# Blocks of attention scores in larger parts where the instruction stream is crowded, and an earlier index for the last batch's left tiles

## The chip, the core and the metric

The kernel runs on one core of one Trainium2 chip. The metric is the device time of one execution in microseconds, lower is better. TensorE (PE; its weight loads are shown as PEld), VectorE (DVE), ScalarE (ACT), GpSimd (POOL) and SyncE (SP, which issues most DMAs) each run their own instructions in program order and wait for each other on semaphores.

## The reference

Agent attention feeds a top-1 mixture of experts, in float32:

```python
def _attn_ref(q, k, v, agents):          # q, k, v: 4 x 11456 x 128, agents: 4 x 49 x 128
    a2k = sm(agents, k)                  # softmax of scaled scores
    agent_v = a2k @ v
    q2a = sm(q, agents)
    return q2a @ agent_v
...
def _moe_ref(x, w_gate, w_output_gate, w1, w2):   # x: 45824 x 128, 8 experts, F = 1024
    logits = x @ w_gate
    e_idx = np.argmax(logits, axis=1)
...
    gate_w = probs[np.arange(N), e_idx]
    eom = 1.0 / (1.0 + np.exp(-(x @ w_output_gate)))
    for e in range(E):
        mask = e_idx == e
...
        h = np.maximum(x[mask] @ w1[e], 0.0)
        ye = h @ w2[e]
        out[mask] = gate_w[mask, None] * eom[mask, e, None] * ye
```

## The kernel before

The tokens of each of the four batches are cut into 12 units (`UNITS`): 11 of 8 times 128 tokens and one of 2 times 96. For every unit there are score products of q with the 49 agents (tiles qs), and of k (ks); with their softmax weights the agents' averages of v are built per batch (ev, av), and from these one expert is chosen for the batch. The main loop then multiplies, for tiles of 512 tokens, the turned attention weights (x_ld) by first-layer weights folded with the averages (h), takes the relu in two float16 halves (hh by ACT, hl by DVE), multiplies by the second layer (y), and DVE or ACT with POOL scales the result into an output tile (os, a ring of four), which SP stores.

Tokens for which the chosen expert or the shortened computation doesn't hold are left over. They are handled in up to 128-token tiles ("left" tiles; `STATIC` reserves 10, 6, 1 and 4 for the four batches): `left_counts` counts them by expert, `left_index` finds on DVE and PE (tiles cums and lis) which tokens belong to each tile and gathers their attention weights from DRAM by an indirect DMA on POOL (big), `left_front` turns them (let) and multiplies by the averages (lx), `left_load` loads the expert's weights on SP (lw, lws), `left_back` runs both layers in fp32 (lh, ly), and `left_store` scatters the rows.

The order of all instructions is set when the kernel is built. Each of these steps is a Python generator that offers its next instruction. `Clock` keeps an estimated time of each engine and of each tile's readiness; `tick` lets an offered instruction into the stream when the clock says that its inputs are there, at most one fp32 product (`heavy`) and two others (`light`) in a turn of the main loop. A block of scores goes in as a whole (`blocked`), when the main loop calls `block`: 8 groups of 128 tokens, each cut into parts of `part[0]` tokens, each part one fp32 product of 50 columns. `PART` is 32, and 64 when the main loop has nothing to do (`idle`). SP's order is set in the same way, so a load that becomes known earlier stands ahead of stores that become ready later.

Names: `bank` and `hold` take a PSUM bank; `SY.wait` and `values_load` bring the expert's number (ei, tile lei) into a register of SP; `got` tells the loader and the front that a left tile is ready.

Of the kernel before, what the change touches and what calls it, by code (L numbers as in the profile page):

```python
# [13 lines left out]
ALU = mybir.AluOpType  # L14
# [4 lines left out]
B, N, C, A, E, F = 4, 11456, 128, 49, 8, 1024  # L19
# [9 lines left out]
NCOL = 90  # L29
# [7 lines left out]
MOST = 5  # L37
# [29 lines left out]
class Clock:  # L67
# [7 lines left out]
    def __init__(self):  # L75
        self.vt = dict.fromkeys(("PE", "ACT", "DVE", "POOL", "SP", "DMA"), 0.0)
        self.ready, self.read, self.writer, self.before = {}, {}, {}, {}
        self.slots = [1, 2, 0]
        self.pe = 0.0
        self.psum = set()  # L80

        self.apart = {"out"}
        self.recent = []
        self.started = False
        self.margin = LANDS
        self.quiet = 0.0

    def now(self):
        return self.vt["PE"]

    def columns(self, t):

# [41 lines left out]
    def issue(self, eng, ins, outs, cost, after):  # L134
        t = max(self.vt[eng], self.at(ins, outs, eng), 0.0 if eng == "PE" else self.now() - 200.0)
        if eng == "PE":
            slow = 1.0 if self.columns(t) >= 3072 else 2.0
            wide = ins[0].dtype == F32
            if wide and _free(ins[0]) > 64:

                t += max(0.0, (66.0 - self.pe) * slow - (t - self.vt["PE"]))
            self.pe = 0.0 if wide else cost
            cost *= slow
            n = _free(outs[0]) * (4 if ins[0].dtype == F32 and ins[0].shape[0] else 1)
            if wide and _free(ins[0]) <= 64:
# [135 lines left out]
def agent_attention_top1_moe(ctx, tc, qT, kT, v, aT, wg, wo, w1, w2, cst, slots, out):  # L281
    nc = tc.nc
    clk = Clock()
# [235 lines left out]
                    break  # L519
        streams[:] = [x for x in streams if x[2] is not None]  # L520

    PART, TURN = 32, 100.0
    part = [PART]

    def block():
# [8 lines left out]
    def blocked(o, pairs, last=None):  # L534

        yield "PE", list(pairs[0][1:]), [o], 2
        clk.vt["PE"] += TURN
        n = len(pairs)
        for i, (t, x, m) in enumerate(pairs):
            w = _free(x)  # L540
            for h in range(0, w, part[0]):
                c = min(part[0], w - h)
                dst = o[h:h + c, :] if last else o[h:h + c, t * A2:(t + 1) * A2]
                PE.matmul(dst, x[:, h:h + c], m, start=(not last or i == 0), stop=(not last or i == n - 1))
        clk.vt["PE"] += 138.0
# [1114 lines left out]
        yield from POOL.q.tensor_copy(nti[b], x[:, 4, E - 1:E])  # L1660
        yield from POOL.q.tensor_scalar(over[:, b:b + 1], x[:, 4, E - 1:E], float(STATIC[b]), None, op0=ALU.is_gt)

    def left_index(b, ti, n, nm, big, got=None):

        x, key = facts[b], keys[b]
        cm = steps[:, 0:n]
# [10 lines left out]
        yield from DVE.q.tensor_reduce(s4, m, axis=AX.X, op=ALU.add)  # L1677
        ei = wk.tile([P, MOST], I32, name=f"lei{nm}", tag="lei", bufs=3)[0:1, 0:n]
        yield from DVE.q.tensor_copy(ei, s4[0:1, :, 3])
        lo, hi = lt("llo", nm, [n, 1])[:, :, 0], lt("lhi", nm, [n, 1])[:, :, 0]  # L1680
        yield from DVE.q.scalar_tensor_tensor(lo, ti, -float(P), s4[:, :, 0], op0=ALU.mult, op1=ALU.add)
        yield from DVE.q.tensor_tensor(hi, lo, s4[:, :, 1], op=ALU.add)
# [10 lines left out]
        bc = [P, n, P]  # L1693
        yield from DVE.q.tensor_tensor(at, iotar.unsqueeze(1).broadcast_to(bc), hi.unsqueeze(2).broadcast_to(bc),
                                       op=ALU.is_lt)
        yield from wait_free()
        t = bank(f"li{nm}")
        mark = hold()
        for k in range(n):
            yield from DVE.q.scalar_tensor_tensor(at[:, k, :], iotar, lo[:, k:k + 1], at[:, k, :], op0=ALU.is_ge,  # L1700
                                                  op1=ALU.mult)
            yield from PE.q.matmul(t[:, k * NCOL:(k + 1) * NCOL], at[:, k, :], cum[:, k, :], start=True, stop=True)
            yield from PE.q.matmul(t[:, MOST * NCOL + 2 * k:MOST * NCOL + 2 * k + 2], at[:, k, :], rowc, start=True,
                                   stop=True)
        tv = t[:, 0:n * NCOL].rearrange("p (n c) -> p n c", c=NCOL)
        tr = t[:, MOST * NCOL:MOST * NCOL + 2 * n].rearrange("p (n c) -> p n c", c=2)
        yield from DVE.q.scalar_tensor_tensor(cum, tv, pcol, colw.unsqueeze(1).broadcast_to([P, n, NCOL]), op0=ALU.is_le,
# [9 lines left out]
        tg = tu  # L1717
# [8 lines left out]
        for k in range(n):  # L1726
            yield from POOL.q.indirect_dma_start(out=ef[:, k, :], out_offset=None, in_=efd[b],
                                    in_offset=bass.IndirectOffsetOnAxis(ap=tu[:, k:k + 1], axis=0),
                                    bounds_check=N - 1, oob_is_err=False)
            if got:  # L1730
                got(k, clk.ready[big.name] + (2000.0 if n > 1 else 0.0), ei, tg, ef, oa)
            yield from pause(1500.0 if n > 1 else 0.0)
        return ei, tg, ef, oa

# [82 lines left out]

    LEFT = 5

    ready, averaged = {}, {}  # L1820
    prepared, stored = [0], [0]
    sets = [(ph, i, n) for ph, x in enumerate(SETS) for i, n in enumerate(x)]

    def left_prepare(b):

        while counted[0] <= b or b > prepared[0]:
            yield None
        yield from left_counts(b)
        averaged[b] = yield from left_averages(b, f"{b}")
        i = 0  # L1830
        for j, n in enumerate(SETS[b]):
            m = sets.index((b, j, n))
            last_ = m == len(sets) - 1
            while not last_ and stored[0] < sum(x[2] for x in sets[:max(m - 1, 0)]):
                yield None
            big = wk.tile([P, n * (A2 + C)], F32, name=f"big{b}_{j}", tag="S3" if last_ else f"lb{m % 2}", bufs=1)

            def got(k, t, ei, tg, ef, oa, i=i):
                ready[b, i + k] = t, ei, k, tg[:, k:k + 1], ef[:, k, :], oa[:, k, :]
            yield from left_index(b, iotar[:, i:i + n], n, f"s{b}_{i}", big, got)  # L1840
            i += n
        prepared[0] += 1

# [7 lines left out]
    def left_static():  # L1851
# [5 lines left out]
        def fronts():  # L1857
            for i, (b, k) in enumerate(todo):
                while (b, k) not in ready or i > finished[0] + 1:
                    yield None  # L1860
                t, _, _, _, ef, _ = ready[b, k]
                yield from pause(t - clk.now())
                fronted[b, k] = yield from left_front(f"{b}_{k}", ef, averaged[b])

        def weights():
            for i, (b, k) in enumerate(todo):
                while (b, k) not in ready or vacant_home() is None:
                    yield None
                home = vacant_home()
                busy[home] = True  # L1870
                _, ei, kk, _, _, _ = ready[b, k]
                loaded[b, k] = home, *(yield from left_load(ei, kk, f"{b}_{k}", home))

        spawn(fronts(), LEFT - 1)
# [1 line left out]
        for b, k in todo:  # L1876
            while (b, k) not in fronted or (b, k) not in loaded:
                yield None
            home, w1t, w2t = loaded.pop((b, k))
            _, _, _, tg, ef, oa = ready[b, k]  # L1880
            yield from pause(clk.ready[w1t.name] - clk.now())
            yield from left_back(f"{b}_{k}", fronted.pop((b, k)), w1t, w2t, oa, ef, home)
            busy["own2" if home == "own" else home] = False
# [125 lines left out]
```

## Time and profile before

| | us |
|---|---|
| three runs | 710.17, 713.03, 717.61 |
| median | 713.03 |
| the profiled execution, its own time | 713.61 |
| span of the profiled execution, first to last instruction | 711.8 |
| PE busy | 650.5 (91%) |
| DVE, ACT, POOL busy | 492.9, 414.7, 277.9 |
| TensorE's granted clock, mean share | 0.963 |

The profile is of one execution. Busy times are unions of an engine's instructions, and an fp32 product shows as two MATMUL and two LDWEIGHTS records. Idle time stands with the instruction that ended it and with what released that; "issue" means that nothing which the profile shows released it. The 1.8 us between the span and the execution's own time lie before the first and after the last instruction.

### The profile page before, as it was taken

Reading aid. Unit: us, or ns where it says so; the run is one execution under the profiler, and the core shown is the slowest. Engines: PE = TensorE matmul, PEld = TensorE weight load, DVE = VectorE, ACT = ScalarE, POOL = GpSimd, SP = SyncE. Lnnn points to the kernel's source line nnn. Section 1 sums busy time; section 2 is a strip of 40 time slices with the busy share of each in tenths; the row PEclk is TensorE's granted clock in tenths of the full one; section 3 lists DMA queues with packets and bytes.
Section 4 is the critical chain, followed back from the end, with each engine's and each line's share of the span. In section 5 each row is a group of like instructions: output and inputs, shape, how many; then the busy total and the mean of one; then the engine's idle time right before and its main releaser. Section 6 shows DMA issues by size and latency. Waiting matters only on the chain.

```text
span 711.8 us, 27564 instructions
## 1 busy us (share of the span) xinstructions
PE 650.5 (91%) x11238; PEld 547.8 (77%) x11238; DVE 492.9 (69%) x1615; ACT 414.7 (58%) x1118; POOL 277.9 (39%) x518
## 2 busy tenths in 40 slices
PE   8999999899985999999877989999899999999983
PEld 7887777678775677878766878788789888898873
DVE  1785657676758788788865757876879877676800
ACT  2442497675654585664664757765655697854321
POOL 3011225368423539323832225574522344331211
PEclk9996999999988799999999999999999999999997
DMA  8988354969989279926379778786976459541450
GB/s 305 360 263 272 104 134 134 276 207 274 272 287 240 86 177 267 285 80 180 114 216 266 210 201 242 216 228 232 275 222 172 134 159 298 156 150 66 154 216 10
DMA packets 98246, 144.86 MB, mean 204 GB/s; under 512 B 54845, under 2 KB 63045, under 8 KB 98112
## 3 DMA queue, kind: packets, MB, share of 16 engines
q1 hardware_dynamic: 96768, 141.71, 68.4%
q0 software_dynamic: 1344, 1.32, 0.9%
q8 instruction: 90, 1.47, 0.9%
q14 instruction: 44, 0.36, 0.2%
HBM read 97.76 MB, written 34.10 MB: 185 GB/s over the span
## 4 chain that ended last, share of the span: by engine, by line
PE 57%; DVE 8%; issue 7%; POOL 4%; ACT 4%; DMA 3%; POOLq 0%; DVEq 0%; ACTq 0%
PE y L231 17%; PE h L231 8%; PE lh L231 6%; PE ly L231 5%; PE qs L231 4%; PE ck L231 4%; PE ks L231 3%; PE av L231 3%; ACT ck L231 2%; POOL sm L231 2%; PE lg L231 1%; DMA x_ld<-e 1%; POOL ev L231 1%; PE lx L231 1%; ACT hh L231 1%
## 5 line engine op out<-in xcount | busy, mean ns | idle before, releaser
L231 PE MATMUL y<-vv,hh 128*128 128x128 f16 (+1 forms) x1440 | 170.0, 220 | 3.0 <-issue 3.0
L231 PEld LDWEIGHTS <-x_ld 128*128 128x128 f16 (+1 forms) x1800 | 132.5, 101 | 48.3 <-issue 18.5
L231 DVE SCALAR_TENSOR_TENSOR hl<-h,hh 128x512 f16<-128x512 f32 (+1 forms) x184 | 119.8, 669 | 50.9 <-ACT hh L231 49.9
L231 PE MATMUL y<-vv,hl 128*128 128x128 f16 x720 | 144.9, 220 | 0.0
L231 ACT ACTIVATE hh<-h 128x512 f16<-128x512 f32 (+1 forms) x184 | 99.3, 583 | 65.3 <-PE h L231 64.6
L231 ACT ACTIVATE ck<-ck 128x512 f32<-128x512 f32 x180 | 106.2, 590 | 21.4 <-PE ck L231 17.7
L231 PEld LDWEIGHTS <-hh 128*128 128x128 f16 (+1 forms) x1440 | 111.7, 100 | 7.6 <-issue 3.3
L231 PE MATMUL y<-gw,x_ld 128*128 128x128 f16 x720 | 86.0, 220 | 9.2 <-ACT ck L231 1.9
L231 PEld LDWEIGHTS <-hl 128*128 128x128 f16 x720 | 73.4, 102 | 1.4
L231 POOL TENSOR_TENSOR e<-ef,e 128x392 f16<-128x392 f32 (+1 forms) x48 | 41.8, 870 | 78.2 <-ACT e L231 75.7
L231 PE MATMUL ck<-wc,x_ld 128*128 128x256 f16 x360 | 69.0, 273 | 3.3 <-DVE avs L231 0.8
L231 PE MATMUL lg<-gs,x_ld 128*128 128x18 f16 x720 | 62.8, 172 | 3.9 <-DMA x_ld<-e 3.6
L231 PE MATMUL h<-x_ld,w 128*128 128x512 f16 (+1 forms) x184 | 63.3, 379 | 2.0 <-DVE hl L231 1.6
L231 PE MATMUL lh<-lxs,lw 128*128 128x128 f32 x288 | 58.2, 300 | 0.4 <-ACT lxs L231 0.4
L231 PE MATMUL ks<-at,k_ld 128*32 128x50 f32 (+1 forms) x2084 | 51.3, 219 | 6.9 <-issue 5.5
L231 PEld LDWEIGHTS qs<-at,q_ld 128*32 128x32 f32 (+1 forms) x2640 | 40.5, 115 | 20.6 <-issue 14.2
L231 PE MATMUL qs<-at,q_ld 128*32 128x50 f32 (+1 forms) x2640 | 49.1, 214 | 7.9 <-issue 7.7
L231 PEld LDWEIGHTS ks<-at,k_ld 128*32 128x32 f32 (+1 forms) x2084 | 44.3, 124 | 14.5 <-issue 9.4
L231 PE MATMUL ly<-lw,lh 128*128 128x128 f32 x288 | 55.3, 298 | 0.0
L231 PE MATMUL h<-x_ld,wr 128*128 128x512 f16 (+1 forms) x184 | 54.4, 378 | 0.0
L231 DVE TENSOR_TENSOR os<-y,smt 128x512 f32<-128x512 f32 (+1 forms) x58 | 38.8, 670 | 20.5 <-PE y L231 15.5
L231 POOL TENSOR_TENSOR ev<-S,km_o 128x400 f32<-128x400 f32 (+1 forms) x36 | 33.0, 915 | 37.1 <-PE av L231 35.7
(269 smaller groups left out, 1397.0 us busy)
## 6 DMA issues: line engine op xcount, KB each, us to landing
v_ld<-v SPq DMA_DIRECT2D x44, 512.0 KB, 5.2
q_ld<-qT SPq DMA_DIRECT2D x44, 512.0 KB, 4.7
out<-os SPq DMA_DIRECT2D x88, 256.0 KB, 3.9
k_ld<-kT SPq DMA_DIRECT2D x43, 512.0 KB, 5.0
lw<-w SPq DMA_DIRECT2D x36, 512.0 KB, 3.9
efd<-ef SPq DMA_DIRECT2D x44, 200.0 KB, 3.3
lws<-w SPq DMA_DIRECT2D x6, 512.0 KB, 6.4
w1t<-w SPq DMA_DIRECT2D x4, 512.0 KB
```

Of the source, the lines that this page charges most:

```text
L231: return getattr(self.eng, op)(*a, **k)
```

## The change

`Clock.crowd` counts the instructions that the order has put on PE in the last 4000 ns of the estimated clock, 4 for an fp32 product and 2 for another. Where this count and 16 for each group of the block come to more than `CROWD`, 285, the block's parts are 64 tokens and not 32. In `left_index`, for the last batch alone, DVE masks all tiles first, and the index products of all tiles go to PE at once as one entry, without a turn of the main loop between them. Also for the last batch, `known` announces the experts' numbers as soon as DVE has them, and the loader of weights waits for `chosen`, which that sets, where it waited for the gather's issue; the 2000 ns that `got` added to the estimated landing of a gather are dropped there.

```diff
+    def crowd(self):
+        while self.given and self.given[0][0] < self.vt["PE"] - 4000.0:
+            self.given.pop(0)
+        return sum(x[1] for x in self.given)
...
             self.pe = 0.0 if wide else cost
+            self.given.append((t, 4 if wide else 2))
...
-    PART, TURN = 32, 100.0
+    PART, TURN, CROWD = 32, 100.0, 285
...
         n = len(pairs)
+        size = part[0] if clk.crowd() + 16 * n <= CROWD else 2 * PART
         for i, (t, x, m) in enumerate(pairs):
             w = _free(x)
-            for h in range(0, w, part[0]):
-                c = min(part[0], w - h)
+            for h in range(0, w, size):
+                c = min(size, w - h)
...
         yield from DVE.q.tensor_copy(ei, s4[0:1, :, 3])
+        if known:
+            known(ei)
...
-        yield from wait_free()
-        t = bank(f"li{nm}")
-        mark = hold()
-        for k in range(n):
+        for k in range(n if b == B - 1 else 0):
             yield from DVE.q.scalar_tensor_tensor(at[:, k, :], iotar, lo[:, k:k + 1], at[:, k, :], op0=ALU.is_ge,
                                                   op1=ALU.mult)
-            yield from PE.q.matmul(t[:, k * NCOL:(k + 1) * NCOL], at[:, k, :], cum[:, k, :], start=True, stop=True)
-            yield from PE.q.matmul(t[:, MOST * NCOL + 2 * k:MOST * NCOL + 2 * k + 2], at[:, k, :], rowc, start=True,
-                                   stop=True)
+        yield from wait_free()
+        t = bank(f"li{nm}")
+        mark = hold()
+        if b == B - 1:
+            yield "PE", [at, cum], [t], 0
+        for k in range(n):
...
+            for x, y in ((t[:, k * NCOL:(k + 1) * NCOL], cum[:, k, :]),
+                         (t[:, MOST * NCOL + 2 * k:MOST * NCOL + 2 * k + 2], rowc)):
+                if b < B - 1:
+                    yield "PE", [at[:, k, :], y], [x], 0
+                PE.matmul(x, at[:, k, :], y, start=True, stop=True)
...
             if got:
-                got(k, clk.ready[big.name] + (2000.0 if n > 1 else 0.0), ei, tg, ef, oa)
+                got(k, clk.ready[big.name] + (2000.0 if n > 1 and b < B - 1 else 0.0), ei, tg, ef, oa)
...
+            def known(ei, i=i, n=n):
+                for k in range(n):
+                    chosen[b, i + k] = ei, k
...
-                while (b, k) not in ready or vacant_home() is None:
+                while (b, k) not in chosen or vacant_home() is None:
                     yield None
                 home = vacant_home()
                 busy[home] = True
-                _, ei, kk, _, _, _ = ready[b, k]
+                ei, kk = chosen[b, k]
```

Where the order of instructions changes: 21 of the 68 rows of score blocks that stood in parts of 32 now stand in parts of 64, at the same places; up to the last batch's left tiles no other row moves. Here is one on PE, near the end of the second batch's main loop, with k scores of the fourth batch. `ks` is the block, `h` and `y` are the main loop. Before:

```order
L231 LDWEIGHTS hl_1_7521
L231 MATMUL y_7756<-vv_4918,hl_1_7521 128x128
L231 MATMUL ks_2_7895<-at,k_2_ld 32x50 x32
L231 LDWEIGHTS w_4968
L231 MATMUL h_0_7939<-x_10_ld,w_4968 128x512
```

and after:

```order
L238 LDWEIGHTS hl_1_7361
L238 MATMUL y_7564<-vv_4758,hl_1_7361 128x128
L238 MATMUL ks_2_7687<-at,k_2_ld 64x50 x16
L238 LDWEIGHTS w_4808
L238 MATMUL h_0_7715<-x_10_ld,w_4808 128x512
```

The block is at its place with 16 products for 32.

On PE in the last batch's main loop, the index products (`lis`), the first of four pairs before:

```order
L231 LDWEIGHTS x_8_ld
L231 MATMUL y_14221<-gw_85,x_8_ld 128x128
L231 MATMUL lis_0_14191<-cums_0_14162 128x90
L231 LDWEIGHTS hh_0_14054
L231 MATMUL y_14221<-vv_11882,hh_0_14054 128x128
L231 LDWEIGHTS hh_0_14054
L231 MATMUL y_14221<-vv_11882,hh_0_14054 128x128
L231 MATMUL lis_0_14191<-kc,cums_0_14162 128x2
L231 LDWEIGHTS hl_0_14055
```

and all four pairs after:

```order
L238 LDWEIGHTS hh_1_13811
L238 MATMUL y_13945<-vv_11562,hh_1_13811 128x128
L238 MATMUL lis_0_13943<-cums_0_13826 128x90
L238 MATMUL lis_0_13943<-kc,cums_0_13826 128x2
L238 MATMUL lis_0_13943<-cums_0_13826 128x90
L238 MATMUL lis_0_13943<-kc,cums_0_13826 128x2
L238 MATMUL lis_0_13943<-cums_0_13826 128x90
L238 MATMUL lis_0_13943<-kc,cums_0_13826 128x2
L238 MATMUL lis_0_13943<-cums_0_13826 128x90
L238 MATMUL lis_0_13943<-kc,cums_0_13826 128x2
L238 LDWEIGHTS hl_1_13812
```

The pairs, which were spread over four turns, stand together, between where the second and the third stood. Further down, the transposes (`let`) and `lx` products of tiles 0 and 1 and two `lh` products of tile 0 move from behind the last `y` product of the main loop to places inside its last 52 `y` products.

On SP in the last batch, stores of the output (`out`) and loads of left weights (`lw`, `lws`), before:

```order
L231 DMA out<-os_14136 128x512
L231 DMA out<-os_14209 128x512
L231 DMA out<-os_14262 128x512
L231 DMA out<-os_14319 128x512
L1737 TENSOR_LOAD leis_0_14143
L231 ISA
L231 DMA lw_0_14417<-w 128x1024
```

and after:

```order
L238 DMA out<-os_13800 128x512
L1755 TENSOR_LOAD leis_0_13807
L238 ISA
L238 DMA lw_0_13863<-w 128x1024
L238 ISA
L238 DMA lw_0_13865<-w 128x1024
L1755 TENSOR_LOAD leis_0_13807
```

The wait for the experts' numbers and the six loads of tiles 0 to 2 move ahead of three stores, and no store stands between the loads any more, where one did.

## Rows read from the trace of the kernel before

**Rows 1.** Page of the kernel before: span, busy times, chain by engine.

```profile
span 711.8 us, 27564 instructions
PE 650.5 (91%) x11238; PEld 547.8 (77%) x11238; DVE 492.9 (69%) x1615; ACT 414.7 (58%) x1118; POOL 277.9 (39%) x518
...
PE 57%; DVE 8%; issue 7%; POOL 4%; ACT 4%; DMA 3%; POOLq 0%; DVEq 0%; ACTq 0%
```

**Rows 2.** Timeline of PEld: start, duration, instruction, count, idle before and releaser.

```profile
129.00 0.10 PEld L231 LDWEIGHTS <-hh 128*128 128x128 f16 x1 [3.17 <-issue]
...
198.01 1.18 PEld L231 LDWEIGHTS ks<-at,k_ld 128*32 128x32 f32 x46 [2.07 <-issue]
...
218.22 0.50 PEld L231 LDWEIGHTS ks<-at,k_ld 128*32 128x32 f32 x36 [0.84 <-issue]
...
374.65 0.41 PEld L231 LDWEIGHTS ks<-at,k_ld 128*32 128x32 f32 x29 [2.79 <-issue]
...
384.72 0.14 PEld L231 LDWEIGHTS qs<-at,q_ld 128*32 128x32 f32 x4 [2.78 <-issue]
...
403.48 0.32 PEld L231 LDWEIGHTS qs<-at,q_ld 128*32 128x32 f32 x19 [1.26 <-issue]
...
413.47 0.23 PEld L231 LDWEIGHTS qs<-at,q_ld 128*32 128x32 f32 x10 [2.40 <-issue]
```

**Rows 3.** Page, DMA queues: the instruction queue of 16 KB packets.

```profile
q8 instruction: 90, 1.47, 0.9%
```

**Rows 4.** Stretches from stall to stall: busy us and instructions by engine, PEclk, DMA.

```profile
374.64:384.71 10.07, 7.43 (x255) 6.00 (x255) 6.08 (x20) 4.42 (x12) 1.68 (x4) 1.00 1.07 237
384.71:403.47 18.76, 17.38 (x382) 14.92 (x382) 11.59 (x32) 13.95 (x40) 5.08 (x10) 1.00 0.87 251
403.47:413.46 9.99, 7.72 (x254) 6.75 (x255) 6.00 (x20) 5.49 (x13) 2.55 (x6) 1.00 0.76 194
```

**Rows 5.** Timeline of PE: two whole blocks of scores.

```profile
189.12 1.14 PE L231 MATMUL ks<-at,k_ld 128*64 128x50 f32 x32 [0.22 <-DVE r L231]
...
192.86 0.91 PE L231 MATMUL ks<-at,k_ld 128*32 128x50 f32 x64
```

**Rows 6.** Stretches, columns as in rows 4: three falls of the clock.

```profile
130.56:133.97 3.41, 3.41 (x36) 3.21 (x34) 1.26 (x3) 1.32 (x4) 1.23 (x2) 0.50 1.05 295
198.83:205.66 6.83, 6.83 (x104) 5.20 (x104) 3.06 (x12) 4.07 (x12) 3.02 (x5) 0.50 0.96 366
413.87:417.28 3.41, 3.41 (x81) 3.16 (x69) 0.46 (x4) 0.86 (x2) 0.00 (x0) 0.50 0.72 192
```

**Rows 7.** Chain that ended last, 184 to 245 us: start, duration, what.

```profile
182.26 8.95 DMA x_ld<-e
```

**Rows 8.** Timeline of PE in the last batch.

```profile
663.00 0.41 PE L231 MATMUL lis<-cums 128*128 128x90 f32 x2
...
666.64 0.41 PE L231 MATMUL lis<-cums 128*128 128x90 f32 x2
...
668.97 0.34 PE L231 MATMUL lis<-kc,cums 128*128 128x2 f32 x2
...
675.10 0.22 PE L231 MATMUL y<-vv,hl 128*128 128x128 f16 x1
...
680.74 0.28 PE L231 MATMUL let<-kc,big 128*49 128x128 f32 x1 [2.41 <-DMA big<-efd,ltus]
...
685.92 2.44 PE L231 MATMUL ly<-lw,lh 128*128 128x128 f32 x16
```

**Rows 9.** Timelines of SP and POOL in the last batch.

```profile
669.64 2.78 SPq L231 DMA_DIRECT2D lw<-w  x4
...
673.34 1.05 POOL L231 DMA_INDIRECT big<-efd,ltus  x1 [10.95 <-issue]
```

**Rows 10.** DMA issues: the gather of left rows, count, median us to landing.

```profile
big<-efd,ltus POOLq DMA_INDIRECT x21, 4.6
```

More of the change, by code (lines that the diff above doesn't have):

```diff
@@ L82, in __init__ @@
         self.apart = {"out"}
-        self.recent = []
+        self.recent, self.given = [], []
         self.started = False
@@ L1661, in left_counts, with left_index @@
         yield from POOL.q.tensor_scalar(over[:, b:b + 1], x[:, 4, E - 1:E], float(STATIC[b]), None, op0=ALU.is_gt)
-    def left_index(b, ti, n, nm, big, got=None):
+    def left_index(b, ti, n, nm, big, got=None, known=None):
         x, key = facts[b], keys[b]
@@ L1695, in left_index @@
                                        op=ALU.is_lt)
+        for k in range(n if b == B - 1 else 0):
+            yield from DVE.q.scalar_tensor_tensor(at[:, k, :], iotar, lo[:, k:k + 1], at[:, k, :], op0=ALU.is_ge,
+                                                  op1=ALU.mult)
         yield from wait_free()
@@ L1698, in left_index @@
         mark = hold()
+        if b == B - 1:
+            yield "PE", [at, cum], [t], 0
         for k in range(n):
-            yield from DVE.q.scalar_tensor_tensor(at[:, k, :], iotar, lo[:, k:k + 1], at[:, k, :], op0=ALU.is_ge,
-                                                  op1=ALU.mult)
-            yield from PE.q.matmul(t[:, k * NCOL:(k + 1) * NCOL], at[:, k, :], cum[:, k, :], start=True, stop=True)
-            yield from PE.q.matmul(t[:, MOST * NCOL + 2 * k:MOST * NCOL + 2 * k + 2], at[:, k, :], rowc, start=True,
-                                   stop=True)
+            if b < B - 1:
+                yield from DVE.q.scalar_tensor_tensor(at[:, k, :], iotar, lo[:, k:k + 1], at[:, k, :], op0=ALU.is_ge,
+                                                      op1=ALU.mult)
+            for x, y in ((t[:, k * NCOL:(k + 1) * NCOL], cum[:, k, :]),
+                         (t[:, MOST * NCOL + 2 * k:MOST * NCOL + 2 * k + 2], rowc)):
+                if b < B - 1:
+                    yield "PE", [at[:, k, :], y], [x], 0
+                PE.matmul(x, at[:, k, :], y, start=True, stop=True)
         tv = t[:, 0:n * NCOL].rearrange("p (n c) -> p n c", c=NCOL)
@@ L1818, in agent_attention_top1_moe @@
     LEFT = 5
-    ready, averaged = {}, {}
+    ready, averaged, chosen = {}, {}, {}
     prepared, stored = [0], [0]
@@ L1838, in got @@
             def got(k, t, ei, tg, ef, oa, i=i):
-                ready[b, i + k] = t, ei, k, tg[:, k:k + 1], ef[:, k, :], oa[:, k, :]
-            yield from left_index(b, iotar[:, i:i + n], n, f"s{b}_{i}", big, got)
+                ready[b, i + k] = t, tg[:, k:k + 1], ef[:, k, :], oa[:, k, :]
+                if b < B - 1:
+                    chosen[b, i + k] = ei, k
+            def known(ei, i=i, n=n):
+                for k in range(n):
+                    chosen[b, i + k] = ei, k
+            yield from left_index(b, iotar[:, i:i + n], n, f"s{b}_{i}", big, got, known if b == B - 1 else None)
             i += n
@@ L1860, in fronts @@
                     yield None
-                t, _, _, _, ef, _ = ready[b, k]
+                t, _, ef, _ = ready[b, k]
                 yield from pause(t - clk.now())
@@ L1879, in left_static @@
             home, w1t, w2t = loaded.pop((b, k))
-            _, _, _, tg, ef, oa = ready[b, k]
+            _, tg, ef, oa = ready[b, k]
             yield from pause(clk.ready[w1t.name] - clk.now())
```

## The prediction

> **What bounds the kernel now.** I read the page first: PE is busy for 650.5 of 711.8 us, the next engine for 492.9 [rows 1]. So the question is what PE does in the other 61 us, and in the busy time that is spent at half clock. In the timeline of the weight loads I looked for idle time that ended with "issue", which means that the profile shows nothing that released it. Seven such stalls stand out, 0.84 to 3.17 us each, 15.3 us together [rows 2]. Six are in the middle of a block of scores (ks or qs), where the products need nothing that the ones just before had not needed.
>
> What they have in common is a count. Between the end of one stall and the end of the next lie 510, 764 and 509 instructions of PE and PEld [rows 4], which is 2, 3 and 2 times 255. The instruction queue moved 1.47 MB in 90 packets, 16 KB each [rows 3], and PE and PEld together ran 22,476 instructions [rows 1], 250 per packet. So I read the stalls as PE having run through one packet of instructions before the next had landed. The two stretches of two packets took 10.07 and 9.99 us for 7.43 and 7.72 us of work [rows 4]: there the supply was one packet in 5.0 us, and the data transfers beside it ran at 237 and 194 GB/s.
>
> After three of these stalls the granted clock is at 0.50, the lower of its two levels (1.2 GHz), for 3.41, 6.83 and 3.41 us [rows 6], and PE is busy all through. That is 13.65 us in which half the work was done: 6.8 us lost.
>
> The end is another stage. PE's main loop ends at 678.33 us (680.74 less 2.41) and PE then waits 2.41 us for the gather of the last batch's left rows [rows 8]. The gather was issued at 673.34, which was after the four pairs of index products had passed PE between 663.0 and 669.3 us, a pair in every turn of the main loop [rows 8, 9].
>
> **The change part by part.** *Parts of 64.* The order shows 21 of the 68 rows of blocks in parts of 32 tokens now in parts of 64; all else in the stages before 655 us stands as before. Four of them belong to the stage from 120 us, six to the next, ten to the third, one stands late. Each drops 16 of its 32 fp32 products, in the trace 64 of 128 records (32 products show as x64, 16 as x32 [rows 5]). The price: a block in parts of 32 takes 0.91 us, one in parts of 64 takes 1.14 [rows 5], so 21 x 0.23 = +4.8 us on PE, with nothing to hide it, since PE is the bound. The Trainium skill ("TensorEngine Tiling (Array Packing)", When to Use Tiling) has 32 columns run four abreast and 64 two abreast, by which both blocks would take the same time and the term would be 0. Rows 5 differ by 0.23 us, and the rows decide.
>
> The gain: the count that runs out is lower. In 374.64 to 384.71 us two blocks are thinned, so 510 - 128 = 382 instructions, at 5.0 us for 255 a supply of 7.5 us; the work is 10.07 - 2.78 + 0.46 = 7.75 us. The stall goes. In 403.47 to 413.46 us, where the second block is cut off by the end, it is 509 - 118 = 391, a supply of 7.7 us against 9.99 - 2.40 + 0.46 = 8.05 us of work; it goes too. In 384.71 to 403.47 us only one block is thinned, and I leave half of the 1.26 us. At 129.00, 198.01, 218.22 and 374.65 us 90 to 160 instructions less lie ahead of the stall, which at some 50 instructions per us (510 in 10.07) puts the packet's end 2 to 3 us later; of 3.17, 2.07, 0.84 and 2.79 us I leave 0.9 us in all. By this 13.8 of 15.3 us go. But every thinned block also moves the ends of all later packets to other places, and a new stall can arise in any crowded block that was not thinned. I take 11 us as gone, with bounds 6 and 15.3.
>
> The falls of the clock each follow a stall, but the stalls that ended at 374.65 and 384.72 us had none. I take two thirds of the 6.8 us: 4.5, bounds 0 and 6.8.
>
> Who is late next? PE gains 11 + 4.5 - 4.8 = 10.7 us, spread over three stages. The chain holds one wait for a turned load of 8.95 us at 182 us [rows 7], so data can become the wait there. DVE is busy for 69% and ACT for 58% [rows 1], which leaves room on average. I keep two thirds: **-7.1 us**.
>
> *Index products in one go.* The order puts the four pairs next to each other, in the main loop about 0.4 us before where the third pair stood (666.64 us). Two pairs no longer stand ahead, at half a microsecond each (0.41 and 0.34 us overlap [rows 8]). So they run from about 665.2 to 667.2 us, not to 669.3: 2.1 us earlier, and DVE has one round of the main loop (two hl and one os) less to do ahead of what follows. The gather then issues at 671.2. It took 7.4 us to its user last time (673.34 to 680.74), while four weight loads were issued at 669.64 [rows 9]; the median of all 21 gathers is 4.6 us [rows 10]. I take 4.6: landed at 675.8.
>
> *Who waits for it now.* The first transpose of the left rows (let) is no longer behind the main loop but inside it, at the place of 675.10 us [rows 8], with 52 products of the loop behind it on PE. It waits 0.7 us. Then both transposes, both lx products and two lh products of the first tiles run inside the loop, 1.3 us more, so the loop ends at 680.3. Six lh products (1.35 us), a relu (0.4) and the 16 ly records of tile 0 (2.0) follow: tile 0 is done at 684.0, before it was at 688.4 (685.92 + 2.44): **-4.4 us**. If the gather takes 7.4 us again, let waits 3.5 us and the gain is 1.6; with no wait it is 5.1. The three tiles behind it and the last scatter cost what they cost.
>
> *Weights when the experts are known.* On SP six loads (3 MB) now stand before stores of the output, no longer between them. SP waits for ei, which DVE has written by then, and with it the stores behind. Nobody waits for these stores until their buffer of four comes round again, some 13 us later. I cost it at nothing; what it brings is the free path of the gather, counted above.
>
> Sum: -7.1 - 4.4 = -11.5 us against the profiled execution's 713.6, which is 0.6 over the median 713.03. On the median: **701.5 us**.
>
> **The rivals.** *The stalls stay* (slower). If a packet is late because the data in flight hold it up, whatever PE has run, it stays late, and the gather, which goes through the same engines, stays at 7.4 us. For it speaks that transfers run at 194 to 251 GB/s in these stretches; against it, that the stalls fall only where 255 instructions pass in about 5 us. Price: +4.8 for the thinned blocks, nothing back, -1.6 at the end: 713.0 + 3.2 = 716.2. It decides once less than 3.2 us of stalls and falls go.
>
> *No instruction was ever late.* The stalls are semaphores or transfers that the profile misses; then 64-token parts cost 4.8 us and only the end gains 4.4: 713.4 us. The Trainium skill has a rule that comes to this ("Runtime: NRT & Kernel Launch", Instruction fetch mechanics): the next block of 16 KiB, 256 instructions, is fetched while the current one runs, and the crossing is mostly hidden. Against it speak six stalls inside blocks [rows 2] and three distances that are multiples of 255 [rows 4].
>
> *PE's lead is taken by the data.* The 8.95 us load at 182 us [rows 7] and its like are issued no earlier, and PE waits for them where it waited for instructions. Then the 10.7 us of the crowded stages shrink to about a third, 3.5, and the end still gains 4.4: 705.1 us; with none kept, 708.6. For it speaks that one load; against it, that PE's other idle time has many small causes and no such wait stands among the seven.
>
> That the change doesn't do what it says is out: the order shows the parts and the places.
>
> **How the numbers follow.** Forecast 0.62, lead taken by the data 0.20, stalls stay 0.13, no instruction late 0.05. The forecast's own range comes from its bounds: stalls and falls that go 6 to 22 us, less 4.8, two thirds kept, and 1.6 to 5.1 at the end, so 710.6 down to 696 and, with all kept, 691. To hold 8 in 10 I take 692 to 712: the case of the data is inside, 716 is not. The three runs of before lie 1% apart, so a change within 1% (706 to 720 us) can't be told from none. Faster by more: most of the forecast (0.55) and some of the data's case (0.11). Within 1%: 0.29. Slower by more: 0.05.
>
> **What would show it.** Right: "issue" before PEld of qs and ks falls from seven waits of about 2 us to one or two; the instruction queue has some 5 packets fewer (21 x 64 / 255); the clock falls once or not at all between 120 and 420 us; PE's busy time there changes little; the let product stands before the end of the main loop, and tile 0's ly ends 4 us after it. Wrong: the same number of stalls at other blocks; or the same idle time of PE, now put down to x_ld, DVE or ACT; or a wait of let in the loop of more than 3 us.

## The result and the profile after

The changed kernel takes 691.87 us (median of 4 runs, 690.14 to 692.40). The kernel before took 713.74 beside it (4 runs, 710.17 to 717.61). The ratio is 0.968, with a 95% interval of 0.964 to 0.972: 21.9 us faster where the prediction had 11.5. The time lies 0.1 us under the predicted range. Of the runs of before beside the experiments three were slow (720.12, 727.71 and 871.86 us); the medians and ratios below leave them out.

The page of the kernel after, with the lines that answer to [rows 1] and [rows 3]:

```profile
span 690.1 us, 26219 instructions
PE 646.4 (94%) x10566; PEld 546.1 (79%) x10566; DVE 491.3 (71%) x1615; ACT 414.4 (60%) x1118; POOL 278.0 (40%) x518
...
q8 instruction: 85, 1.39, 0.8%
...
PE 60%; DVE 8%; issue 4%; ACT 4%; POOL 4%; DMA 2%; POOLq 0%; ACTq 0%; SPq 0%; DVEq 0%
```

PE is busy 4.1 us less, the span is 21.7 us shorter. So most of the gain was idle time of PE, and "issue" has gone from 7% of the chain to 4%. The instruction queue moved 85 packets where it moved 90.

To place the gain, take three products that both orders hold. First the kernel before, timeline of PE: the first block that the change thins, the first ck behind the third crowded stage, the last tile's ly.

```profile
120.84 0.92 PE L231 MATMUL ks<-at,k_ld 128*32 128x50 f32 x64
...
417.12 0.46 PE L231 MATMUL ck<-wc,x_ld 128*128 128x256 f16 x2
...
698.82 2.05 PE L231 MATMUL ly<-lw,lh 128*128 128x128 f32 x16
```

The same three in the kernel after:

```profile
118.65 1.14 PE L238 MATMUL ks<-at,k_ld 128*64 128x50 f32 x32
...
400.28 0.38 PE L238 MATMUL ck<-wc,x_ld 128*128 128x256 f16 x2
...
677.30 2.05 PE L238 MATMUL ly<-lw,lh 128*128 128x128 f32 x16
```

The stretch between the first two shrank from 296.28 to 281.63 us: **-14.65 in the crowded stages**. From there to the last ly it went from 281.70 to 277.02: **-4.68 at the end**. The other -2.19 lie ahead of 120 us, where both orders are the same, instruction for instruction. In the ten profiles below that start alike, this block began between 117.99 and 121.43 us, so this part is put down to the chance of the two profiled executions.

What happened inside the first stretch is in the windows view (us; busy us and instructions of PE, PEld, DVE, ACT, POOL; granted clock; DMA share; GB/s). Before, then after:

```profile
120.84:417.12 296.28, 261.31 (x5283) 215.27 (x5282) 218.61 (x706) 182.41 (x494) 139.26 (x235) 0.95 0.78 213
```

```profile
118.65:400.28 281.63, 259.77 (x4644) 215.36 (x4643) 217.07 (x705) 182.09 (x494) 139.63 (x235) 0.97 0.79 222
```

PE has 639 records less, which is 20 blocks of 32, and hardly less to do (-1.54 us): the dearer blocks took back most of what the clock gave. Its idle time went from 34.97 to 21.86 us. Of the seven stalls of [rows 2] one is left, in the block where before waited at 384.72, and a small new one stands further on, in the timeline of PEld:

```profile
371.50 0.20 PEld L238 LDWEIGHTS qs<-at,q_ld 128*64 128x64 f32 x4 [0.74 <-issue]
...
385.51 0.36 PEld L238 LDWEIGHTS ks<-at,k_ld 128*64 128x64 f32 x9 [0.56 <-issue]
```

Of the three falls of the clock of [rows 6] none is left. Two stretches at 0.50 remain in these stages, and one of them is new. The first stands at the end of the second stage, where before had one that [rows 6] leave out; the second had no counterpart. Before, then after:

```profile
226.13:239.78 13.65, 8.22 (x46) 4.75 (x47) 12.92 (x57) 2.47 (x10) 6.44 (x13) 0.50 0.46 127
```

```profile
216.66:230.31 13.65, 9.33 (x68) 5.30 (x72) 12.31 (x51) 3.58 (x13) 6.72 (x14) 0.50 0.40 91
329.30:332.71 3.41, 3.41 (x15) 1.71 (x13) 1.63 (x9) 0.72 (x2) 2.59 (x5) 0.50 0.30 102
```

The end, timelines of PE, SP and POOL, as in [rows 8, 9]:

```profile
648.63 0.41 PE L238 MATMUL lis<-cums 128*128 128x90 f32 x2
...
650.22 0.31 PE L238 MATMUL lis<-kc,cums 128*128 128x2 f32 x2
...
658.70 0.27 PE L238 MATMUL let<-kc,big 128*49 128x128 f32 x1
...
664.83 2.01 PE L238 MATMUL ly<-lw,lh 128*128 128x128 f32 x16
```

```profile
641.94 2.43 SPq L238 DMA_DIRECT2D lw<-w  x4
...
654.20 1.05 POOL L238 DMA_INDIRECT big<-efd,ltus  x1 [8.39 <-issue]
```

The index products run in 1.9 us, the gather issues at 654.20, and 4.5 us later the first let runs inside the main loop without any idle time ahead of it; before it was 7.4 us, with a wait of 2.41. The weights went out 12 us ahead of the gather, not 4 us.

### The profile page after: what moved, and what is told of

Read it like the earlier page. It is cut to its first block, busy times and chain, and to the rows that moved or that the text cites. A ratio compares the mean times of both kernels' runs of the same rounds, so it can differ in the third digit from the quotient of the medians.

```text
span 690.1 us, 26219 instructions
## 1 busy us (share of the span) xinstructions
PE 646.4 (94%) x10566; PEld 546.1 (79%) x10566; DVE 491.3 (71%) x1615; ACT 414.4 (60%) x1118; POOL 278.0 (40%) x518
## 3 DMA queue, kind: packets, MB, share of 16 engines
q0 software_dynamic: 1344, 1.32, 0.8%
## 4 chain that ended last, share of the span: by engine, by line
PE 60%; DVE 8%; issue 4%; ACT 4%; POOL 4%; DMA 2%; POOLq 0%; ACTq 0%; SPq 0%; DVEq 0%
PE y L238 19%; PE h L238 8%; PE lh L238 5%; PE ly L238 5%; PE ck L238 4%; PE qs L238 4%; PE ks L238 4%; PE av L238 3%; ACT ck L238 2%; DVE hl L238 1%; PE lg L238 1%; ACT hh L238 1%; DMA out<-big,ltgs 1%; POOL sm L238 1%; PE lis L238 1%
## 5 line engine op out<-in xcount | busy, mean ns | idle before, releaser
L238 PEld LDWEIGHTS <-x_ld 128*128 128x128 f16 (+1 forms) x1800 | 131.0, 100 | 46.4 <-issue 17.6
L238 PE MATMUL ks<-at,k_ld 128*64 128x50 f32 (+1 forms) x1636 | 51.9, 221 | 1.2 <-issue 0.4
L238 PEld LDWEIGHTS ks<-at,k_ld 128*64 128x64 f32 (+1 forms) x1636 | 45.4, 131 | 8.2 <-issue 3.5
```

Source lines behind the costliest of these rows:

```text
L238: return getattr(self.eng, op)(*a, **k)
```

## Experiments

Twelve kernels ran in three sets of four; each set shared its chip and its runs of before. Before took 717.80, 719.65 and 714.36 us (medians) in the three sets, and 713.74 beside the result, so ratios are to be read within a set. Times within one profile are of one execution, which is not always near the median: the profiles of E1, E4, E5, E9 and E12 are of the longest of their runs, those of E6, E7 and E8 of the shortest.

**E1: the parts of 64 alone.** Index products and weights of the last batch as before.

```
-        for k in range(n if b == B - 1 else 0):
...
-        if b == B - 1:
-            yield "PE", [at, cum], [t], 0
...
-        if known:
-            known(ei)
```

> The kernel before with the parts of 64 tokens alone; index products and weights of the last batch as before. Theory A (the crowded stages gave 17.5 us, since the stalls go whole and with them the falls of the clock, and the end gave the 4.4 us that the prediction worked out): 713.7 - 17.5 = 696.3 us, with at most one 'issue' stall of over 0.7 us before a block of scores, no fall of the clock between 120 and 210 us and none at 414 us, and a wait of 2 to 3 us of let behind the main loop. Theory B (the end gave the larger half, the crowded stages the 7.1 us of the prediction): 706.6 us.

Measured: 704.62 us, 0.981 (0.977 to 0.985) of 717.80, so -13.2. As a share of before, theory A comes to 0.976 and theory B to 0.990: the interval holds neither. The signs that A named for the crowded stages came: one stall of over 0.7 us, no fall of the clock from 122 to 216 us or at 414. From the first block that the change thins to the ck behind the third stage this profile takes 284.00 us; E2, of the same set and with these blocks in parts of 32, takes 303.81. The total is 8 us above A's: before itself is 4.1 us slower here, and of the gain 4 us are missing. In the profiled execution, the longest of the four, PE lost the clock at the end:

```profile
670.79:681.03 10.24, 9.54 (x49) 8.47 (x47) 1.27 (x4) 2.24 (x6) 0.00 (x0) 0.50 0.43 155
```

That fall costs some 5 us there; the other three executions, at a mean granted clock of 0.970 to 0.975 where this one has 0.966, have no profile. The last products of the main loop ahead of it had waited some tenths of a microsecond each; let ran in it at 672.23, 7.9 us behind the gather's issue, with no wait of its own.

**E2: the end alone.**

```
-        size = part[0] if clk.crowd() + 16 * n <= CROWD else 2 * PART
+        size = part[0]
```

> The changed kernel with all blocks in parts of 32 as before, so only the last batch's index products in one go and its weights early. Theory A: the end alone gives 4.4 us, 709.3 us, with the seven stalls and three falls of the clock at the same blocks as before. Theory B (the end gave the larger half): 699 us, about 14.8 us less than before.

Measured: 717.93 us (712.61 to 720.41), 0.998 (0.994 to 1.001). Theory B is out; the 4.4 us of theory A are just inside the interval, no more. What the run shows well is that the stalls keep their places: eight "issue" waits in the crowded stages, 16.9 us together, six of them before the very products of [rows 2]. Three of these six, PEld:

```profile
127.94 0.10 PEld L238 LDWEIGHTS <-hh 128*128 128x128 f16 x1 [3.30 <-issue]
...
378.46 0.41 PEld L238 LDWEIGHTS ks<-at,k_ld 128*32 128x32 f32 x29 [2.24 <-issue]
...
389.35 0.19 PEld L238 LDWEIGHTS qs<-at,q_ld 128*32 128x32 f32 x4 [3.64 <-issue]
```

**E3: every full block in parts of 64.**

```
+        size = 2 * PART
```

> The changed kernel with every full block of scores in parts of 64: 36 more blocks lose half of their products. Theory A (a block in parts of 64 costs 0.23 us more of PE whether crowded or not, and instructions are scarce only in the places already thinned): 691.9 + 36 x 0.23 = 700.2 us, less 0.7 us for the one stall left. Rival (the wider part costs nothing where PE has idle time beside it, or nothing at all): 691 us, and if fewer instructions help everywhere, 689.

Measured: 708.07 us, 0.987 (0.983 to 0.990). The changed kernel came to 0.977 on the like (E5). The difference, 0.0103 of 718 us, is 7.4 us where theory A had 7.6. This agreement is a weak one, since the two stand in different sets and the changed kernel itself came to 0.968 and 0.970 in others. The price rests on the blocks: in E3's profile 75 whole blocks at the full clock take 1.14 us (median) in parts of 64, in that of before 47 take 0.91 in parts of 32. So a block costs its 0.23 us wherever it stands, and no gain from the 36 further blocks shows. The queue's packets fell to 76 with the instructions.

**E4: all packets moved by half.** 128 instructions at the start, otherwise the kernel before.

```
         PE.matmul(bank(f"warm{i}")[:, 0:P], idle_w, idle_w, start=True, stop=True)
+        for _ in range(2 if i < 32 else 0):
+            PE.eng.matmul(bank(f"warm{i}")[:, P:P + 2], idle_w, idle_w[:, 0:2], start=True, stop=True)
```

> The kernel before with 64 products of two columns (128 instructions of PE and its weight loads) put between the warming products at the start; all work and its order behind them as before. Their results are not used. Theory A (PE waits at the ends of instruction packets): the stalls leave their places; each stands 128 instructions earlier in the program (or 128 later, half a packet), none before the same product as before, and their number and sum are drawn anew, 5 to 20 us, so 706 to 720 us. Rival (a semaphore, a transfer of data or the buffers hold the products up): the same seven stalls before the same products, and 713.7 us within 1.5.

Measured: 727.99 us, 1.014 (1.010 to 1.018). My forecast of the time missed because the short products were not cheap: 0.22 us each, 14 us in all (the second ks block starts at 23.83, before at 9.38). Without these 14 us it is some 4 us under before. The places decide: no stall stands before a product of [rows 2]. PEld (left out are 2.44 us at 371.96 before a load of x_ld, 0.91 at 216.01, 0.74 at 410.19, and the end of the second stage, where before waits too):

```profile
140.95 0.21 PEld L231 LDWEIGHTS ks<-at,k_ld 128*32 128x32 f32 x8 [2.79 <-issue]
...
200.70 0.10 PEld L231 LDWEIGHTS <-hh 128*128 128x128 f16 x1 [1.29 <-issue]
...
205.31 0.14 PEld L231 LDWEIGHTS ks<-at,k_ld 128*32 128x32 f32 x3 [0.80 <-issue]
...
228.53 0.45 PEld L231 LDWEIGHTS qs<-at,q_ld 128*32 128x32 f32 x33 [0.79 <-issue]
...
232.17 0.77 PEld L231 LDWEIGHTS ks<-at,k_ld 128*64 128x64 f32 x22 [0.85 <-issue]
...
390.44 0.45 PEld L231 LDWEIGHTS ks<-at,k_ld 128*32 128x32 f32 x33 [1.22 <-issue]
...
396.92 0.10 PEld L231 LDWEIGHTS <-w 128*128 128x128 f16 x1 [2.13 <-issue]
...
424.87 0.10 PEld L231 LDWEIGHTS <-w 128*128 128x128 f16 x1 [1.88 <-issue]
...
428.34 0.23 PEld L231 LDWEIGHTS ks<-at,k_ld 128*32 128x32 f32 x11 [0.81 <-issue]
```

And the stretches from stall to stall hold 255, 258 and 255 records of PE and PEld, and 1273 in the long one, about 5 times 255 (a window also counts what reaches over its edges; from stall to stall it is 254, 254, 254 and 1272):

```profile
200.71:205.31 4.60, 3.94 (x128) 3.55 (x127) 2.13 (x7) 2.30 (x6) 0.00 (x0) 1.00 0.91 299
228.54:232.18 3.64, 2.86 (x129) 2.64 (x129) 2.44 (x10) 2.13 (x6) 0.00 (x0) 1.00 0.55 164
396.92:424.75 27.83, 25.50 (x637) 22.15 (x636) 17.44 (x58) 18.15 (x51) 7.66 (x16) 0.94 0.94 229
424.75:428.34 3.59, 2.92 (x128) 2.24 (x127) 1.70 (x3) 2.24 (x6) 0.00 (x0) 1.00 0.76 205
```

Same work, same order, same data, and the waits went to other products at the same spacing. That is theory A; a semaphore or a load would have stayed with its product.

The traces also hold the packets themselves. In the kernel before, DMA view of 371.8 to 372.0 us, one starts just when PE has stopped at 371.86:

```profile
q8 instruction: 1, 0.02, 46.1%
```

The packet's own time, 46.1% of what 16 engines have in 0.2 us, is 1.48 us, so it lands 1.3 us ahead of 374.65, where the stall ends. All seven stalls of [rows 2] end 1.2 to 1.5 us behind the landing of such a packet, and the eleven waits of over 0.7 us in E4 that keep the spacing 1.2 to 1.6 us. From the stall at 129.00 to that at 413.47 PE and PEld run 9912 instructions while 39 packets land, 254 for each. So these waits end with a packet of instructions; the count alone had only suggested it. The seven late packets took 0.93 to 1.48 us, all 90 of them 0.88 to 1.76: what was late is their start, not their way.

**E5: the changed kernel once more,** unaltered, in the second set.

> The changed kernel, word for word, once more, because the parts alone (0.981 of before) and the end alone (0.998) together give only 0.979 and not its 0.968. Theory A (the two terms add, and the chips differ in how much before loses to stalls): the ratio comes out at 0.972 to 0.980 where before takes some 718 us. Theory B (each part needs the other): 0.968 again, whatever before takes.

Measured: 703.30 us (701.07 to 705.50), 0.977 (0.973 to 0.980): -16.4. Theory A: E1's 1.9% and E2's 0.2% of before come near these 2.3%. The change was worth 22 us beside the result and 16 here.

**E6: index products in one go, weights late.** The loader waits for the gather's issue again.

```
-            yield from left_index(b, iotar[:, i:i + n], n, f"s{b}_{i}", big, got, known if b == B - 1 else None)
+            yield from left_index(b, iotar[:, i:i + n], n, f"s{b}_{i}", big, got)
```

> The changed kernel, but the last batch's left tiles ask for their weights only when their rows have been gathered, as before; the index products stay in one go, the blocks of scores in their two sizes. Theory A (the early loads cost and bring nothing; the end gains by the index products): within 0.7 us of the changed kernel. Theory B (the early loads bring the gain, since the first lh products wait for their weights): 3 to 5 us slower than the changed kernel, with an lh product that waits for lw.

Measured: 706.62 us, 0.981 (0.977 to 0.985), 3.3 us above E5 in the same set, and at the ratio of E1, which has neither but stands in another set. The medians lie as theory B said, but not for its reason: no lh product waits for weights. It is let that waits, after the gather; POOL and PE:

```profile
661.77 1.05 POOL L238 DMA_INDIRECT big<-efd,ltus  x1 [8.39 <-issue]
...
667.64 0.28 PE L238 MATMUL let<-kc,big 128*49 128x128 f32 x1 [2.09 <-remote]
```

From issue to let it is 5.9 us, right behind and beside the weights (SP issues them from 657.03 to 662.53), and let, now inside the main loop, waits 2.09 us. The ranges of E5 and E6 overlap (701 to 705.5, 702 to 707), so the time alone doesn't settle it. The profiles show less: take the stretch from the main loop's 280th y product from its end to the start of the last tile's ly, whose first 20.03 us are alike in all kernels. It lasts 46.72 us in E6 and 45.67 in E5, 1.05 less, and 47.47 in E7, of the same set, which has the old end.

**E7: only the third stage thinned.**

```
+        size = part[0] if mains[0] < 40 or clk.crowd() + 16 * n <= CROWD else 2 * PART
```

> The kernel before with parts of 64 in the eleven crowded blocks from 365 us on alone, none in the two stages ahead, and the end as before. Theory A (what PE gains in the crowded stages is kept nearly whole): four stalls of 9.2 us go and a fall of the clock worth 1.7 us, 11 blocks cost 0.23 us each: 8.4 us faster than before on this chip, while the three stalls and two falls ahead of 230 us stay. Theory B (two thirds are kept, as the prediction had it): 5.6 us. Theory C (a stage that gains hands its gain to the next wait): under 3 us.

Measured: 712.54 us, 0.990 (0.987 to 0.994), -7.1: between A (8.4) and B (5.6), which the interval (4.5 to 9.5) doesn't part; C is out. In the stages ahead of 230 us the stalls stayed, as they should, and yet the clock didn't fall behind them, which theory A had wrong:

```profile
126.26 0.10 PEld L238 LDWEIGHTS <-hh 128*128 128x128 f16 x1 [2.51 <-issue]
...
131.64 1.07 PEld L238 LDWEIGHTS ks<-at,k_ld 128*64 128x64 f32 x17 [1.32 <-issue]
...
407.67 0.43 PEld L238 LDWEIGHTS ks<-at,k_ld 128*64 128x64 f32 x11 [1.38 <-issue]
```

The last row, in a block that is thinned, is not in the traces of the changed kernel; E8 has it too. Thinning less ahead of a place moves the packet ends there as well.

**E8: fewer blocks.** `CROWD` 330, 14 blocks instead of 21.

> The changed kernel with the bound of a crowded place raised from 285 to 330, so 14 blocks are in parts of 64 and 7 of the 21 go back to parts of 32. Theory A (each block in parts of 64 costs 0.23 us and the seven were not needed): 7 x 0.23 = 1.6 us faster than the changed kernel. Rival (two or three stalls of some 2 us come back in the stages from 180 and 365 us): 3 to 5 us slower.

Measured: 707.57 us, 0.984 (0.981 to 0.987), 4.3 us above E5. The rival holds: three waits came back, 1.46 us at 196.56, 1.15 at 389.80 and 1.20 at 406.07, and behind the first a fall of 3.41 us.

**E9: weights early, index products a pair in a turn.** The branches for `b == B - 1` in `left_index` are taken out, `known` stays.

> The changed kernel with the last batch's index products one pair in a turn again, as before, and only its weights loaded early; the blocks of scores in their two sizes. With the parts alone (0.981 of before), the index products in one go (0.981) and both (0.977) this makes the square whole. Theory A (the early loads bring the whole gain of the end, because the gather no longer shares its way with them): as fast as the changed kernel within 1 us, and a gather of 4 to 5 us to its first user. Theory B (the early loads and the index products are each worth nothing alone, since the gather comes in time only with both): 3 to 4 us slower than the changed kernel.

Measured: 692.74 us, 0.971 (0.964 to 0.977), against 692.29 of the changed kernel in the same set (E12). Theory A. The gather issues later, let comes later, and nothing is lost, POOL and PE:

```profile
658.75 1.06 POOL L238 DMA_INDIRECT big<-efd,ltus  x1 [10.95 <-issue]
...
663.58 0.27 PE L238 MATMUL let<-kc,big 128*49 128x128 f32 x1
```

From issue to let it is 4.8 us, and let waits for nothing. The stretch named at E6 takes 44.91 us here, 44.19 in E12 and in the result, 49.13 before. The DMA issues view of 640 to 695 us gives the median of the last batch's four gathers from issue to landing (of those whose landing the trace holds, three in E6, four in the others shown). Before, the result, E6, then E9:

```profile
big<-efd,ltus POOLq DMA_INDIRECT x4, 6.1
...
big<-efd,ltus POOLq DMA_INDIRECT x4, 2.6
...
big<-efd,ltus POOLq DMA_INDIRECT x4, 5.4
...
big<-efd,ltus POOLq DMA_INDIRECT x4, 2.8
```

E1 and E7, which load the weights late as well, have 5.8 and 5.2; E12 has 2.5. It is low in just those kernels that load the weights early.

**E10: time put back where the change took it.**

```
+        if mains[0] < 55 and part[0] == PART and size > PART:
+            for _ in range(5):
+                PE.eng.matmul(o[:, 0:2 * P], idle_w, idle_x, start=True, stop=True)
```

> The changed kernel with five products of 256 columns put ahead of each of the twenty blocks that it has in parts of 64 in the crowded stages; their results are written over and not used. At 0.107 us each (128 columns took 0.105 us at half clock) that is 10.7 us of TensorE put where the change took its time out. Theory A (the crowded stages are bound by TensorE throughout, so what is gained or lost there is kept whole): 9 to 11 us slower than the changed kernel. Theory B (a third is taken by waits for data, DVE and ACT, as the prediction had it): 7 us slower. Theory C (most is taken up): under 4 us.

Measured: 702.86 us, 10.6 above E12. What was put in, in the timeline of PE ahead of one block:

```profile
124.83 0.71 PE L549 MATMUL ks<-idle_x 128*128 128x256 f16 x5
125.47 1.14 PE L238 MATMUL ks<-at,k_ld 128*64 128x50 f32 x32
```

From the five products to the block behind them it is 0.64 us. The whole stretch, from the first thinned block (with what stands ahead of it) to the ck behind the third stage, in E10 and then in E12:

```profile
119.20:410.91 291.71, 271.61 (x4744) 224.59 (x4743) 218.60 (x705) 181.98 (x493) 138.61 (x234) 0.97 0.78 215
```

```profile
120.26:403.15 282.89, 260.12 (x4643) 216.53 (x4642) 219.15 (x704) 182.07 (x493) 138.92 (x234) 0.97 0.79 221
```

PE is busy 11.5 us more. Two stalls of E12 (0.82 and 1.12 us) are gone in return, so 9.5 went in net, and 8.8 came out in these profiles, 10.6 in the medians (700.56 to 704.40 against 690.82 to 695.16): theory A, nearly the whole is kept.

**E11: more blocks.** `CROWD` 262, 25 blocks.

> The changed kernel with the bound of a crowded place lowered from 285 to 262: 25 blocks in parts of 64 instead of 21. Theory A (21 is about where cost and gain meet; four more cost 0.9 us and take away one or two stalls of 0.9 us): within 1 us of the changed kernel. Rival (each block thinned in a crowded stage still gains): 2 us faster. Rival (all but the first twenty are pure cost and move packet ends to worse places): 2 us or more slower.

Measured: 692.72 us against 692.29: theory A, no difference.

**E12: the changed kernel, third time.**

> The changed kernel, word for word, as the measure for the three beside it. On a chip where before takes some 718 us: 0.974 to 0.980 of it; where before takes some 713 us: 0.966 to 0.972.

Measured: 692.29 us (690.82 to 695.16), 0.970 (0.964 to 0.976), the absolute time of the result again, with before at 714.36. No version tried is clearly faster than the changed kernel.

## Why the prediction was right in kind and too small

**What failed is the sum for the crowded stages: the mechanism was right, two of its sizes were not.** "I take 11 us as gone" was too little for the stalls, of which some 14 went; and the step "Who is late next?" kept two thirds of a gain of 10.7 us, 7.1, where the profiles show 14.65. Of the 7.5 us missed here some 4.5 lie in the terms, the stalls above all, and 3 in the discount.

- *Stalls.* "I take 11 us as gone", out of 15.3. Of the seven one wait of 0.74 us is left, 14.6 gone; with the new one of 0.56 us it is 14.0 net. The fear that packet ends would move into other crowded blocks was sound in kind (E4, E7 and E8 show just that), but the 20 thinned blocks seem to have left too few instructions for it: E1, E5, E9 and E12 have one or two waits of 0.7 to 1.1 us there. The step-by-step sum for each stall, which came to 13.8, was better than the caution put on it. Its supply of one packet in 5.0 us is what two stretches showed and no fixed rate: before, two packets start 3.5 us apart (401.19 and 404.69 us). That 13.8 came so near is in part luck.
- *Falls of the clock.* 4.5 taken, out of 6.8; all three went, and a new one at 329.30 us took some 1.7 back, so 5.1. The size was near, by chance more than by reason. E7 kept stalls of 2.51 and 1.32 us without a fall, so a stall makes a fall likely and not certain.
- *The price.* 20 blocks in this stretch at 0.22 to 0.23 us make 4.4 to 4.6, as predicted; the first thinned block shows 1.14 where it was 0.92, as do the blocks of E3. The Trainium skill's rule ("TensorEngine Tiling (Array Packing)", When to Use Tiling), by which both parts would cost the same, isn't what these rows show.
- *The discount.* 14.6 + 5.1 - 4.5 = 15.2 us, and 14.65 arrived: 96%, not two thirds. E10 asked the question by itself: a net 9.5 us put into these stages cost 8.8 in the profiles and 10.6 in the medians. So there was hardly any slack behind PE. The prediction argued from one load of 8.95 us in the chain and from the shares of DVE and ACT; it had itself noted that no wait of that kind stood among the seven. I had read a discount into the sum for which no row spoke.

Without the discount and with the stalls as worked out one by one, the sum would have been 13.8 + 4.5 - 4.8 + 4.4 = 17.9 us, which makes 695.1.

**The end** was right in size, -4.4 against -4.68, and wrong in its cause. The sum had the index products bring the gather forward by 2.1 us and the early weights at "nothing". By the stretch named at E6, which took 49.13 us before and 44.19 in the result, the early weights alone (E9, 44.91, in another set) bring 4.2 of the 4.9 us; in the second set the index products alone bring 0.75 (47.47 in E7, 46.72 in E6) and the weights on top of them 1.05, with gathers of 2.2 us (one landing in the trace) for 5.4. So the loads are the lever: with them 12 to 15 us ahead, the gather had its user 4.5 and 4.8 us later in the result and E9, without a wait; issued within 5 us of them, it kept let waiting until 5.9 us from its issue in E6 and 7.4 before. The prediction did name "the free path of the gather", but booked it under the index products. What went is the wait of 2.41 us and the fall of the clock that began at 683.52 (3.41 us, 1.7 lost): 4.1 of the 4.7. The size holds for this pair of profiles only: from E7 to E5 the same stretch gained 1.8 us, from E1, with its fall of 10.24 us, to E2 6.0.

**The remaining 2.2 us** belong to no step; they lie ahead of the first changed instruction. Without them the time would have stood inside the range, whose lower end of 692 left out the 691 that the prediction's own bounds gave with all kept.

**The rivals.** "The stalls stay" and "no instruction was ever late" are out: the stalls went, E4 shows them at distances of about 255 records wherever the work stands, and each ends just behind the landing of a packet. The Trainium skill ("Runtime: NRT & Kernel Launch", Instruction fetch mechanics) says that a crossing is mostly hidden. With 90 packets and seven late ones in the crowded stages "mostly" is right, and 15 us lie in the rest. "PE's lead is taken by the data" fell with E10 for these stages. In the second set there is something to it: E5 took 11.4 us more than the result with the same instructions, partly in waits of ck, of which this is one:

```profile
354.87 0.38 PE L238 MATMUL ck<-wc,x_ld 128*128 128x256 f16 x2 [2.30 <-ACT lh L238]
```

But all eight kernels of the first two sets wait there, thinned or not (1.2 to 2.3 us; 2.3 in E2 with all its stalls), so it wasn't the lead of PE that was taken.

**What it was to show** came in the main: one issue wait of over 0.7 us where seven stood (six of them before qs or ks), five packets fewer (90 to 85), PE's busy time there only 1.5 us less, let inside the main loop. Two signs were off. The clock was to fall once or not at all between 120 and 420 us, and it falls twice, because the fall at the end of the second stage, which stood there before, had not been counted. And tile 0's ly was to end 4 us after the loop: the loop ends at 663.6, ly at 666.8, 3.2 us.

## What to carry to other kernels

Where idle time of the busiest engine ends with "issue", count the instructions of that engine between the ends of such waits: equal distances (here multiples of some 255 of PE and PEld), and a packet of the instruction queue that lands just ahead of the end of each wait (here 1.2 to 1.5 us), show that it ran out of instructions. In such places fewer, larger instructions were worth more here than cheaper ones. A discount on a gain of the bounding engine needs a row for it; if there is none, put a known delay in that place and see what comes out at the end, as E10 did. Keep large loads out of the stretch just ahead of a gather that someone waits for: issued 12 us ahead of it they cost nothing that a run shows.

## What was unexpected

The same program took 691.9 and 692.3 us in two sets of runs and 703.3 in another, while before moved only from 714 to 720. Part of it was seen in E5: waits of 2.42 and 2.30 us ahead of two ck products, at 294.61 and 354.87, where the result has none over 1 us and 1.56, and a fall of the clock behind the second:

```profile
357.28:364.11 6.83, 6.83 (x76) 5.83 (x74) 2.92 (x11) 2.58 (x9) 0.00 (x0) 0.50 0.68 194
```

Every kernel of the first two sets has both waits (1.7 to 2.4 and 1.2 to 2.3 us), whatever was changed in it; before beside the result and the four of the third set have neither over 1 us. Why those sets are slower there stays open. Open as well is what delays a packet: the traces show that it starts late, not why, and whether a fall follows a stall differs between traces of the same stretch (E2 has two ahead of 205 us, E7 none).

A product of two columns at the start took 0.22 us in E4, 64 of them 14 us; a short product is no free way to add instructions.
